# Gated attention and hash-routed experts on one core: routing in smaller parts, fetches at fixed steps, experts' matrices prepared from the third batch on

## The chip, the cores and the metric

The kernel runs on one core of one Trainium2 chip. A core has a matrix engine (PE, with its weight loads shown as PEld), a vector engine (DVE), an activation engine (ACT), a general engine (POOL) and a sync engine (SP); SP, ACT and POOL also issue the DMAs here, each in its own program order. The metric is the device time of one execution in microseconds (us). Before the change three runs gave 2499.6, 2501.89 and 2503.09 us, median 2501.89 us.

## The reference: what is computed

Two stages. The attention has 8 batches of 2496 positions, with no softmax; its output, 19968 rows of 256, is the input of the second stage, in which each row goes through one of 8 experts, chosen by the low three bits of its token's number (the hash's factor leaves 1 when divided by 8).

```python
scores = (1/S) * z @ z.T            # z: 8 x 2496 x 64
attn   = maximum(scores, 0) ** 2
x      = u * (attn @ v)             # u, v: 8 x 2496 x 256
# x as 19968 x 256
expert = token_ids % 8
out[expert == e] = maximum(x[expert == e] @ w1[e], 0) @ w2[e]   # 256 -> 1024 -> 256
```

## The kernel before

**Attention.** The sequence is cut in halves and each half in five groups of up to 256 positions. A step is one triple (batch b, group g of queries, tile s of keys): 25 steps for a batch, 200 in all, numbered i from 0. `STEPS` gives the order of s for each g, and pos = i % 5 is the place of a step in its group. A step makes the scores (`score`, L237: four matmuls of z at L250, ReLU and squares on ACT at L254 to L263, and on DVE at L259 on the diagonal), forms four sums of them on DVE (`sums`, L274 to L277), and multiplies them with v by the seven products of a two-by-two block scheme (`attend`, L325, 28 matmuls). Scores are symmetric. So a tile above the diagonal is also transposed on DVE (`mirror`, L290), written to HBM by SP (`keep`, L298 and L302), and read back by ACT's queue (`recall`, L306) instead of being computed when its mirror image is due. Scores and sums are made two steps ahead of their product (`AHEAD`), recalls are issued three ahead.

**Joins.** The seven products of a group collect over its five steps in four PSUM tiles, and there are only four such tiles. At pos 4 `join` reads them: ACT copies one product (L336), and DVE adds in seven instructions (L338 to L344). The next group's first product can't start before L336 and L338 are done.

**From a group to sorted rows.** One step after a join `gate` turns the result (L356); at pos 1 `put` stores it to HBM (SP, L363, four DMAs) and adds it to the list `waiting`. When the routing is known, `fetch` reads a waiting group back (SP: L371 or L375, and u at L222, three or four DMAs), `multiply` multiplies it by u five steps later (DVE, L388, four instructions), and `sort` writes each row to its slot with indirect DMAs (POOL, L410, four for a group). Of the buffers for u there are two, of those for the rows three.

**Next batch's z.** During a batch SP loads the next one's z in four pieces (`load_z`, L165, at steps 5, 9, 13 and 17 of the batch). Five steps after each load DVE turns the piece (`turn_z`, L185 and L187), and one step later SP copies it to the other half of the partitions (`copy_z`, L192, the last at step 23).

**Routing.** `places` is a generator: each `next` runs it to the following `yield`. It counts the rows of every expert, and gives every row a slot in blocks of 512, 256 or 128 rows of one expert. From step 5 on one part runs at the end of each step, 23 parts, the last at step 27. Only then do fetches begin, at any step with fewer than two groups in flight. From step 32 on one `enter` (POOL, L637) a step writes the token numbers into the slots, 160 in all.

**Experts' matrices.** Each of 16 half experts gets its sums for the seven products. `prepare` loads it (POOL, L659), adds on DVE in two parts of two instructions (L667 to L681), and stores it (POOL, L683); this starts at step 28 and repeats every ten steps, with the parts 0, 4, 5 and 7 steps after the load.

**The second stage** (from 1469 us) runs 60 blocks through the experts; the change touches nothing in it.

The order of instructions on each engine is the order in which this program issues them. At the end of a step it is: scores and sums for two steps on, `keep`, z, `attend`, `join`, `mirror`, v, `gate`, `put`, then routing or `multiply`, `sort` and `fetch`, then `enter` and `prepare`.

Of the kernel before, what the change touches and what calls it, by code (L numbers as in the profile page):

```python
# [24 lines left out]
def kernel(  # L25
# [12 lines left out]
    B, S, D = u.shape  # L38
    K = z.shape[-1]
    N = B * S  # L40
    E, _, F = moe_w1.shape
# [11 lines left out]
    BLK, MID = 512, 256  # L53
    TB, TM = BLK // P, MID // P
    NL = -(-(N - E * (BLK - 1)) // BLK)
    NM = -(-(N - NL * BLK - E * (MID - 1)) // MID)
# [10 lines left out]
    NT = -(-HS // (2 * P))  # L67
# [19 lines left out]
    C = B * 2 * T  # L87
# [342 lines left out]
    def places():  # L430

        with tc.tile_pool(name="route", bufs=1) as route:
# [137 lines left out]
            for size, spare, limit, name in ((BLK, 0, NL, "large"), (MID, 0, NM, "mid"), (P, P - 1, NR, "small")):  # L570
                n, end = share(count, size, spare, limit, name)
                more = route.tile([P, E], F32, name=name + "_more")
# [17 lines left out]
                if size == MID:  # L590
                    yield
# [3 lines left out]
            for (_, _, end), b0, nb in zip(levels, (0, NL, NBIG), (NL, NM, NR)):  # L595
                over = upto[0:1].rearrange(flat_e)[:, 0:nb * E].rearrange('p (j e) -> p j e', e=E)
                nc.vector.tensor_tensor(
                    over, end[0:1, :].unsqueeze(1).to_broadcast([1, nb, E]),
                    iota_b[:, 0:nb].unsqueeze(2).to_broadcast([1, nb, E]), op=OP.is_le)
                eb = route.tile([1, max(NL, NM, NR)], F32, name="eb")  # L600
                nc.vector.tensor_reduce(eb[:, 0:nb], over, axis=AX.X, op=OP.add)
                nc.vector.tensor_scalar(eb_i[:, b0:b0 + nb], eb[:, 0:nb], float(E - 1), None, op0=OP.min)
            nc.vector.tensor_tensor(eb_i[:], eb_i[:], most_i[0:1].to_broadcast([1, NB]), op=OP.bitwise_xor)
# [163 lines left out]
    PER = NG * NT  # L767
# [19 lines left out]
    PREP, PERIOD = 28, 10  # L787
# [12 lines left out]
    for i, (b, g, s) in enumerate(steps):  # L800
# [48 lines left out]
        if i >= 5 and not is_routed:  # L849
            is_routed = next(routed, True) is True  # L850
            if is_routed:

                rowpool = attention.enter_context(tc.tile_pool(name="rowpool", bufs=2))
        elif is_routed:
# [6 lines left out]
            if len(fetched) < 2 and waiting and (len(waiting) > 1 or i > put_at + 1):  # L861
                fetched.append((i, fetch(*waiting.pop(0))))
        if is_routed and 0 <= i - 32 < C:
            enter(i - 32)
        for part, after in enumerate((0, 4, 5, 7)):
            k, due = divmod(i - PREP - after, PERIOD)
            if not due and 0 <= k < 2 * E:
                prepare(k, part)
# [8 lines left out]
    assert is_routed and not waiting and not fetched  # L877
# [216 lines left out]
```

## Time and profile before

| what | value |
|---|---|
| median of three runs | 2501.89 us |
| the profiled execution's own time | 2505.98 us |
| its span (first to last instruction) | 2504.2 us |
| PE busy | 2474.7 us, 99% of the span |
| DVE, ACT, POOL busy | 1735.6, 722.8, 551.5 us |
| attention, about 14 to 1469 us | PE busy 1439.63 of the 1452 us from 17 to 1469 |
| a full step's 28 matmuls | 6.24 us in the chain (5.5 us in the fifth group, which is shorter) |

In a timeline each line has start, duration, engine, line, operation, what is written and read, and the number of instructions; in brackets stands how long the engine idled before it, and what ended that. A table by stretches gives busy time of each engine, then the TensorE clock that was granted (1.00 is full), the mean share of the 16 DMA engines, and GB/s. The step that runs at a time is found by counting L325's groups of 28 from 17 us on: step 20 starts at 169.0 us, step 30 at 243.1, step 45 at 353.0, step 50 at 392.6, step 70 at 541.7, step 100 at 755.1, step 125 at 935.7.

### The profile page before, as it was taken

The numbers are of one execution on the slowest core, as the hardware profiler recorded it, in microseconds if no ns is written. First come the engines' busy times: TensorE is split into PE (matmuls) and PEld (weight loads), VectorE is DVE, ScalarE is ACT, GpSimd is POOL, SyncE is SP. The second block draws the span as 40 slices with busy tenths as digits, with TensorE's granted clock in tenths as the row PEclk, the third lists the DMA queues.
The fourth block names the chain that finished last, engine by engine and source line by source line (L and its number), as shares of the span: only waits on it lengthen the run. The fifth ranks groups of instructions, "written<-read, shape, count | busy, mean of one in ns | idle before, by whom it ended". The sixth has DMA issues, their size and how long they took to land.

```text
span 2504.2 us, 37751 instructions
## 1 busy us (share of the span) xinstructions
PE 2474.7 (99%) x13751; PEld 2114.1 (84%) x13751; DVE 1735.6 (69%) x3686; ACT 722.8 (29%) x1231; POOL 551.5 (22%) x532
## 2 busy tenths in 40 slices
PE   8999999999999999999999999999999999999998
PEld 6787787787787787787777889999999999999998
DVE  7799768768768778778777666655665565556554
ACT  4314314314324224223233112222222222222221
POOL 0000243233313322332233211111111111121212
PEclk9999999999999999999999999999999999999999
DMA  7765798788788687797787776867676767667672
GB/s 147 181 177 161 209 283 235 200 266 220 215 247 228 204 255 201 236 268 195 236 251 210 240 248 208 281 213 215 205 256 192 263 193 252 211 228 232 213 247 75
DMA packets 437292, 550.70 MB, mean 220 GB/s; under 512 B 256908, under 2 KB 368861, under 8 KB 418928
## 3 DMA queue, kind: packets, MB, share of 16 engines
q1 hardware_dynamic: 377328, 363.19, 51.3%
q10 hardware_dynamic: 32448, 97.86, 11.4%
q0 software_dynamic: 27328, 87.23, 9.8%
q8 instruction: 108, 1.77, 0.3%
q14 instruction: 80, 0.66, 0.1%
HBM read 371.36 MB, written 173.24 MB: 217 GB/s over the span
## 4 chain that ended last, share of the span: by engine, by line
PE 87%; DMA 5%; DVE 5%; issue 1%; SPq 1%; ACT 0%; ACTq 0%; POOL 0%; POOLq 0%; DVEq 0%
PE acc L325 40%; PE o_ps L970 17%; PE h_ps L939 17%; PE s_ps L250 8%; PE h_ps L993 3%; PE o_ps L1004 3%; DMA a<-scores 2%; DMA zn<-in_z_dram 1%; DMA u_sb<-in_u_dram 1%; DVE mirror L290 1%; DVE t L274 1%; DVE t L276 0%; DVE t L275 0%; DMA v_sb<-in_v_dram 0%; DVE x_row L388 0%
## 5 line engine op out<-in xcount | busy, mean ns | idle before, releaser
L254 ACT ACTIVATE a<-s_ps 128x512 f32<-128x512 f32 (+1 forms) x480 | 246.6, 598 | 752.5 <-PE s_ps L250 730.1
L325 PEld LDWEIGHTS acc<-a,v_sb 128*128 128x128 f32 (+1 forms) x1600 | 294.6, 190 | 130.3 <-issue 44.5
L325 PE MATMUL acc<-t,vc 128*128 128x256 f32 (+3 forms) x1600 | 404.0, 375 | 0.0
L325 PE MATMUL acc<-a,v_sb 128*128 128x256 f32 (+3 forms) x1600 | 385.0, 383 | 9.6 <-DVE o L338 9.3
L410 POOL DMA_INDIRECT x_slots<-x_row,row x160 | 193.4, 1209 | 810.4 <-DVE x_row L388 671.8
L325 PE MATMUL acc<-t,v_sb 128*128 128x256 f32 (+3 forms) x1600 | 369.7, 373 | 0.0
L325 PEld LDWEIGHTS acc<-t,vc 128*128 128x128 f32 (+1 forms) x1600 | 304.5, 191 | 34.4
L325 PEld LDWEIGHTS acc<-t,v_sb 128*128 128x128 f32 (+1 forms) x1600 | 303.4, 190 | 33.7
L274 DVE TENSOR_TENSOR t<-a 128x512 f32<-128x512 f32 (+1 forms) x200 | 134.2, 671 | 228.6 <-ACT a L263 162.6
L939 PE MATMUL h_ps<-xs,w 128*128 128x256 f32 (+1 forms) x1248 | 288.4, 361 | 0.0
L970 PEld LDWEIGHTS o_ps<-w,h 128*128 128x128 f32 x2272 | 277.0, 192 | 7.9 <-DVE ro L903 1.2
L891 POOL DMA_INDIRECT out_dram<-o_sb,idx x142 | 143.4, 1010 | 629.9 <-issue 406.9
L970 PE MATMUL o_ps<-w,h 128*128 128x128 f32 x2272 | 280.4, 276 | 0.6 <-DVE ro L903 0.6
L250 PE MATMUL s_ps<-zT 64*128 64x512 f32 (+1 forms) x960 | 244.8, 623 | 10.8 <-DVE zT L185 8.0
L946 ACT ACTIVATE h<-h 128x512 f32<-128x512 f32 (+1 forms) x234 | 138.5, 592 | 352.8 <-DVE h L909 141.3
L939 PEld LDWEIGHTS h_ps<-xs,w 128*128 128x128 f32 x1248 | 208.2, 191 | 16.3
L290 DVE STREAM_TRANSPOSE mirror<-a 128x256 f32<-128x256 f32 x640 | 218.0, 407 | 2.0 <-DMA scores<-mirror 2.0
L939 PE MATMUL h_ps<-xT,w 128*128 128x256 f32 (+1 forms) x936 | 213.8, 361 | 2.5 <-DVE h L909 2.5
L970 PEld LDWEIGHTS o_ps<-w,hs 128*128 128x128 f32 x1704 | 206.9, 192 | 4.9
L970 PE MATMUL o_ps<-w,hs 128*128 128x128 f32 x1704 | 209.3, 275 | 0.0
L325 PE MATMUL acc<-a,vc 128*128 128x256 f32 (+3 forms) x800 | 202.0, 375 | 0.0
L637 POOL DMA_INDIRECT slot_tokens<-token,addr x160 | 168.1, 1051 | 65.9 <-issue 47.5
(177 smaller groups left out, 2638.6 us busy)
## 6 DMA issues: line engine op xcount, KB each, us to landing
w<-w_blocks SPq DMA_DIRECT2D x78, 1792.0 KB, 11.1
scores<-mirror SPq DMA_DIRECT2D x192, 256.0 KB, 4.4
a<-scores ACTq DMA_DIRECT2D x48, 1024.0 KB, 4.9
scores<-mirror SPq DMA_DIRECT2D x224, 128.0 KB, 3.8
a<-scores ACTq DMA_DIRECT2D x32, 896.0 KB, 5.7
w_blocks<-w POOLq DMA_DIRECT2D x16, 1792.0 KB, 7.6
w1s<-in_moe_w_dram SPq DMA_DIRECT2D x21, 1024.0 KB, 9.8
w2s<-in_moe_w_dram SPq DMA_DIRECT2D x21, 1024.0 KB, 16.4
```

The costliest lines, as they stand in the source:

```text
L250: nc.tensor.matmul(flat(ps)[:, 0:2 * w].rearrange("p (q c) -> p q c", q=2), tile_of_keys(b, h, s, j), q_h, start=True, stop=True)
L254: nc.scalar.activation(of[:, :, j, h].rearrange("p m q e -> p q m e"), flat(ps)[:, 0:2 * w].rearrange("p (q m e) -> p q m e", q=2, e=in_bl ...
L274: nc.vector.tensor_sub(t1, y12, y11)
L290: nc.vector.transpose(to, in_blocks(a, g)[:, :, j, h].rearrange("p i q (r t) -> p t i q r", t=2)[:, t])
L325: nc.tensor.matmul(acc[k][:, half, 0:w], x[0:n, j, :], y[0:n, j], start=(first and j == 0 and half == 0), stop=(last and j == 1), skip_gro ...
L410: st = nc.gpsimd.indirect_dma_start(out=x_dram[:, :], out_offset=bass.IndirectOffsetOnAxis(ap=row[0:m, c:c + 1], axis=0), in_=x_sb[0:m, q, ...
L637: st = nc.gpsimd.indirect_dma_start(out=slot_dram[:, None], out_offset=bass.IndirectOffsetOnAxis(ap=addr[0:n, to:to + 1], axis=0), in_=tok ...
L891: st = nc.gpsimd.indirect_dma_start(out=out[:], out_offset=bass.IndirectOffsetOnAxis(ap=idx[:, col:col + 1], axis=0), in_=o, in_offset=Non ...
L939: nc.tensor.matmul(ps[:, r], w1[j][:, k, ts(f + r, P)], y, start=first and r == 0, stop=True, skip_group_check=True)
L946: lambda o, i, k, ps=None: nc.scalar.activation(o, o if ps is None else ps, AF.Relu))
L970: nc.tensor.matmul(ps[:, t], x[:, f, ts(t, P)], w2_block(w2[j], k)[:, f], start=first and t == 0 and f == 0, stop=f == FQ - 1, skip_group_ ...
L993: nc.tensor.matmul(ps[:, i, :], w1[j][:, c, ts(f + i, P)], x[:, 0, c, 0:P], start=(c == 0), stop=(c == DP - 1))
```

## The change

Three things change in the order of the work; each engine gets the same instructions.

1. The routing is cut into 27 parts instead of 23 (a `yield` more after the first share, after each of the three sizes, and inside the loop over blocks). A part runs only at steps that are neither pos 4 nor in the first group of a batch: steps 5 to 8, 10 to 13, 15 to 18, 20 to 23, 30 to 33, 35 to 38 and 40 to 42. So the routing ends at step 42 instead of 27.
2. A waiting group is fetched only at steps 1, 5, 8, 12, 15, 19 and 22 of a batch (up to the last 25 steps, where the old rule holds). `multiply` still follows five steps later. `enter` starts when the routing is done and runs once a step, twice at pos 2.
3. `prepare` starts at steps -1, 3 and 8 of each batch from the third on (49, 53, 58, 74, ...), its parts 0, 3, 4 and 6 steps after that.

```diff
--- before.py
+++ after.py
@@ -569,6 +569,8 @@
             levels, base, added = [], 0, None
             for size, spare, limit, name in ((BLK, 0, NL, "large"), (MID, 0, NM, "mid"), (P, P - 1, NR, "small")):
                 n, end = share(count, size, spare, limit, name)
+                if limit == NL:
+                    yield
                 more = route.tile([P, E], F32, name=name + "_more")
                 nc.vector.tensor_sub(more[:], end[:], n[:])
                 nc.vector.tensor_scalar(more[:], more[:], float(size), float(base), op0=OP.mult, op1=OP.add)
@@ -587,8 +589,7 @@
                     nc.vector.tensor_add(next_first[:], first[:], taken[:])
                     first = next_first
                 base += limit * size
-                if size == MID:
-                    yield
+                yield
 
 
 
@@ -600,6 +601,8 @@
                 eb = route.tile([1, max(NL, NM, NR)], F32, name="eb")
                 nc.vector.tensor_reduce(eb[:, 0:nb], over, axis=AX.X, op=OP.add)
                 nc.vector.tensor_scalar(eb_i[:, b0:b0 + nb], eb[:, 0:nb], float(E - 1), None, op0=OP.min)
+                if nb == NM:
+                    yield
             nc.vector.tensor_tensor(eb_i[:], eb_i[:], most_i[0:1].to_broadcast([1, NB]), op=OP.bitwise_xor)
             nc.vector.tensor_scalar(eb_i[:], eb_i[:], E - 1, None, op0=OP.bitwise_and)
 
@@ -784,7 +787,13 @@
     LOAD_V = {-8: 0, -4: 1, -3: 2, -1: 3, 0: 4}
     ADD_V = {-5: 0, -2: 1, -1: 2, 1: 3, 2: 4}
     routed, is_routed = places(), False
-    PREP, PERIOD = 28, 10
+
+
+
+    ROUTE = [i for i in range(len(steps)) if i % NT != NT - 1 and i % PER not in range(NT)]
+    PREPARE = sorted(b * PER + x for b in range(2, B) for x in (-1, 3, 8))[:2 * E]
+    FETCH = (1, 5, 8, 12, 15, 19, 22)
+    entered = 0
     def prepare_mirror(i, a):
         if i < len(steps) and steps[i][2] > steps[i][1]:
             mirrors.append((*steps[i], mirror(*steps[i][1:], a)))
@@ -846,9 +855,10 @@
             late = closing["late"].enter_context(tc.tile_pool(name="late", bufs=1, side="right", reuse_waits="tile"))
             for j in range(SURE):
                 load_x(j)
-        if i >= 5 and not is_routed:
+        if i in ROUTE and not is_routed:
             is_routed = next(routed, True) is True
             if is_routed:
+                assert i < PREPARE[0] - 1
 
                 rowpool = attention.enter_context(tc.tile_pool(name="rowpool", bufs=2))
         elif is_routed:
@@ -858,14 +868,15 @@
                 to_sort += [(*rows, k) for k in range(4)]
             for _ in range(min(2, len(to_sort))):
                 sort(*to_sort.pop(0))
-            if len(fetched) < 2 and waiting and (len(waiting) > 1 or i > put_at + 1):
+            if len(fetched) < 2 and waiting and (i % PER in FETCH or i >= len(steps) - 5 * NT) and (len(waiting) > 1 or i > put_at + 1):
                 fetched.append((i, fetch(*waiting.pop(0))))
-        if is_routed and 0 <= i - 32 < C:
-            enter(i - 32)
-        for part, after in enumerate((0, 4, 5, 7)):
-            k, due = divmod(i - PREP - after, PERIOD)
-            if not due and 0 <= k < 2 * E:
-                prepare(k, part)
+        for _ in range((1 + (i % NT == 2)) * is_routed):
+            if entered < C:
+                enter(entered)
+                entered += 1
+        for part, after in enumerate((0, 3, 4, 6)):
+            if i - after in PREPARE:
+                prepare(PREPARE.index(i - after), part)
         if i == len(steps) - 20:
             load_w(0, 0)
         if i == len(steps) - 2:
@@ -874,7 +885,7 @@
             load_u(b, g)
         if i == len(steps) - 4:
             load_u(b, g, late)
-    assert is_routed and not waiting and not fetched
+    assert is_routed and not waiting and not fetched and entered == C
     for _ in range(len(to_sort)):
         sort(*to_sort.pop(0))
 
```

## The prediction

> **What bounds the kernel now.** I read the page first, then busy time by stretches, then PE's timeline for its idle stretches, then what DVE and SP did ahead of them.
>
> ```profile
> PE 2474.7 (99%) x13751; PEld 2114.1 (84%) x13751; DVE 1735.6 (69%) x3686; ACT 722.8 (29%) x1231; POOL 551.5 (22%) x532
> ...
> PE 87%; DMA 5%; DVE 5%; issue 1%; SPq 1%; ACT 0%; ACTq 0%; POOL 0%; POOLq 0%; DVEq 0%
> ```
>
> ```profile
> 17.00:1469.00 1452.00, 1439.63 (x6553) 1140.39 (x6553) 1122.84 (x2502) 449.39 (x709) 379.56 (x347) 1.00 0.77 221
> ...
> 1490.00:2494.00 1004.00, 1003.42 (x7065) 949.70 (x7064) 591.56 (x1142) 257.59 (x497) 158.92 (x158) 1.00 0.67 221
> ```
>
> PE is the bound, and the change takes no matmul away. The second stage stands still for 0.6 us in 1004. All that can be won is idle time of PE in the attention, 1452 - 1439.63 = 12.4 us, and what a lowered clock adds. These are its idle stretches:
>
> ```profile
> 124.75 1.14 PE L250 MATMUL s_ps<-zT 64*128 64x512 f32 x4 [0.68 <-ACT a L254]
> 169.01 2.47 PE L325 MATMUL acc<-a,v_sb 128*128 128x224 f32 x8 [2.52 <-DVE o L338]
> 243.06 1.99 PE L325 MATMUL acc<-a,v_sb 128*128 128x256 f32 x8 [0.70 <-DVE o L338]
> 352.99 2.15 PE L325 MATMUL acc<-a,v_sb 128*128 128x224 f32 x8 [2.05 <-DVE o L338]
> 388.87 3.75 PE L250 MATMUL s_ps<-zT 64*128 64x512 f32 x6 [2.11 <-DMA zT<-zT]
> 541.65 1.78 PE L325 MATMUL acc<-a,v_sb 128*128 128x224 f32 x8 [1.26 <-DVE o L338]
> 755.07 1.99 PE L325 MATMUL acc<-a,v_sb 128*128 128x256 f32 x8 [0.82 <-DVE o L338]
> 935.66 1.99 PE L325 MATMUL acc<-a,v_sb 128*128 128x256 f32 x8 [1.01 <-DVE o L338]
> 1262.33 1.78 PE L325 MATMUL acc<-a,v_sb 128*128 128x224 f32 x8 [0.78 <-DVE o L338]
> ```
>
> All but the first and the zT one are joins: PE waits for L338, which stands behind other work in DVE's order. Three of them are followed by a slow clock (the last three columns: granted clock, DMA share, GB/s):
>
> ```profile
> 170.00:174.00 4.00, 4.00 (x14) 3.68 (x13) 3.86 (x7) 0.00 (x0) 0.00 (x0) 0.58 0.56 147
> 354.00:358.00 4.00, 4.00 (x15) 3.63 (x14) 3.86 (x10) 0.00 (x0) 3.08 (x4) 0.57 0.75 280
> 388.00:392.00 4.00, 3.13 (x6) 1.20 (x6) 3.93 (x13) 1.05 (x2) 3.09 (x4) 0.55 0.72 169
> 392.00:396.00 4.00, 4.00 (x11) 2.85 (x11) 3.52 (x11) 2.64 (x4) 2.03 (x3) 0.60 1.03 373
> ```
>
> A clock of 0.58 over 4 us loses (1 - 0.58) x 4 = 1.7 us; the others lose 1.7, and 1.8 + 1.6 = 3.4. Idle stretches of 2.05 us and more had it, those of 1.26 and less had not.
>
> Now what stood ahead. At 352.99 and 541.65 it was a `multiply` at pos 3 that waited for its u, at the zT stall a crowded SP queue:
>
> ```profile
> 346.86 0.43 DVE L388 TENSOR_TENSOR x_row<-x_row,u_sb 128x256 f32<-128x256 f32 x1 [2.60 <-DMA u_sb<-in_u_dram]
> 349.03 0.68 DVE L680 TENSOR_TENSOR w<-w 128x512 f32<-128x512 f32 x1
> ...
> 533.34 0.77 DVE L185 STREAM_TRANSPOSE zT<-zn 64x256 f32<-64x256 f32 x2 [4.37 <-DMA zn<-in_z_dram]
> 537.15 0.43 DVE L388 TENSOR_TENSOR x_row<-x_row,u_sb 128x256 f32<-128x256 f32 x1 [2.76 <-DMA u_sb<-in_u_dram]
> ```
>
> ```profile
> 364.76 5.85 SPq L371 DMA_DIRECT2D x_row<-x  x1
> 370.72 3.35 SPq L222 DMA_DIRECT2D u_sb<-in_u_dram  x2
> 376.66 0.47 SPq L192 DMA_DIRECT2D zT<-zT  x1
> ```
>
> **The change part by part.** The instructions of each engine are the same; only places differ, so each term is an idle stretch that goes, stays or comes.
>
> *Routing.* Ahead of 169.01 DVE ran the shares of step 17 and, from 161.37 to 166.29, those of step 18 and the block numbers: 4.9 us of instructions of 0.17 to 0.41 us, then sums, then L338 at 168.54, while PE was free at 166.5. Now step 17 has the scan (L541, 2.78 us) and step 18 one addition (L544, 1.45 us); the shares lie at 20 to 23, the block numbers at 30 and 31. From step 15 to this join DVE has about 26.5 us by its rows (sums 2.2 to 2.7 each, a mirror 2.7, the join's rest 2.8, the routing 6.3), PE about 34 (five products of 6.24 us and two sets of scores). The stall goes: -2.5 - 1.7 = **-4.2**. The last part (L625, 2.37 us, and four small ones), which sat ahead of the join at 243.06, goes to step 42, with a step free before its join: **-0.7**. At step 24 L338 had 1.1 us to spare; the four parts at 20 to 23 are 8.5 us against 5.8, but DVE idled 2.6 us at 199.5 before it: 0 to +1.5, I take +0.3. The three counting rounds move from steps 12, 13, 14 to 13, 15, 16; each holds two score banks until DVE has copied them, and now two rounds stand ahead of a step with scores, not one: **+0.7**, one more stall like that at 124.75 (0 to +1.4).
>
> *Fetches.* In steps 28 to 48 nine fetches were issued; now there are two, at 44 and 47. So no `multiply` stands ahead of the join at 352.99, and no preparing addition (L680, L681: 1.3 us): -2.05 - 1.7 = **-3.8**. The zT copy of step 48 had fetches 38, 39, 43 and 44 ahead of it on SP, of which one took 5.85 + 3.35 = 9.2 us there; now it has 44 and 47: -2.11 - 3.4 = **-5.5**.
>
> Later, `multiply` leaves pos 18 and 23, the steps ahead of the last two joins of a batch: it runs at 6, 10, 13, 20 and 24 (there after the join), and while the backlog lasts (eight groups at step 42, seven fetches a batch against five new groups, so to about step 133) at 2 and 17 too. A `multiply` is 1.43 us by its row, and its wait for u 2.76 at 537.15. The stalls at 541.65, 755.07, 935.66 and 1262.33 and 0.2 at 574.84: 1.26 + 0.82 + 1.01 + 0.78 + 0.2 = **-4.1**. Joins at step 14 keep their `multiply` at 13 and their 0.3 us.
>
> What is late next: seven fetches a batch put more on SP, and SP's DMAs share completion semaphores with ACT's, so some wait for recalls issued later in the program. In the changed order the store before `load_z` of step 63 (and 88, 113) waits for the recall of step 68; before it waited for v of step 67. In this profile that recall was issued at 524.02 and let SP on at 532.09, against 525.67 for the load. It should come sooner, at 529 to 532, with no z load beside it; z takes 6 to 7 us; DVE then needs 1.1 (L185, L187), 2.2 (sums) and 0.4 (L338): 539 to 543, where PE is ready at 540.4. So 0 to 2.6 us, and 1.7 of clock from about 2 on, at each of three joins: I take **+1.0** in all, near the low end, since DVE has lost the `multiply` there (ends 0 and +13). Its like at the batch's end: fetch 22 now stands right before the last zT copy (23). That copy lands 2.6 to 2.8 us after issue where nothing stands before it, 4.6 to 6.7 behind a fetch, and the fetch adds 1.5 us on SP (565.74 to 567.18). Before, it was issued at 563.56, 746.80 and 924.48, and PE's scores need it at about 572.7, 752.3 and 932.7. So 569.7 to 571.8, 752.9 to 755.0, 930.6 to 932.7: in time twice, late by 0.6 to 2.7 once. **+1.5** (0, to 9 each as the rival below). The recall of step 96, which was nearly late for its product (sums at 742.2, product at 746.8), hangs on SP's stores and keeps some of the 0.8 at 755.07: **+0.7** (0 to 2.5).
>
> *Preparing.* The additions move to steps 2, 3, 6, 7, 11 and 12, before joins that had 1.3 to 4.7 us to spare, so 0 (to +1.3, one pair of additions). The load has three steps, not four, before the first addition: 24 us, against a POOL queue that ran up to a step behind (313.6, step 39, for a load of step 38) and 7.6 us to land its like. POOL's `enter` moves from 32 to 191 to 42 to 174: POOL is 22% busy, nothing of PE waits for it.
>
> *Sum.* Gone: 4.2 + 0.7 + 3.8 + 5.5 + 4.1 = 18.3. Come: 0.3 + 0.7 + 1.0 + 1.5 + 0.7 = 4.2. Net -14.1 us: the profiled execution goes from 2505.98 to 2491.9. That execution was 4.1 us above the median, so on the median 2501.89 - 14.1 = **2487.8**.
>
> [...] Here 2.05 to 2.52 us idle were enough for a slow stretch. [...] The DMA engines were 0.98 busy from 375 to 395, when fetches crowded. [...]
>
> **Rivals.** *The fetches' crowd only moves.* In each of batches 2 to 4 the zT copy or the z of step 13 is late as at 388.87. For it: the semaphores above. Against: 7 fetches in 25 steps, not 9 in 21. With 4 us for each of three batches beyond my terms: 2488 + 12 = 2500, the same. *Slower: fetch 22 blocks the copy.* If it costs SP the 9.2 us of 364.76 and not 1.5, the copy lands 9.2 + 2 to 4 = 11 to 13 us later, against 2.8 to 4.6 to spare: 7 to 10 us idle and 1.7 to 3.4 of clock, say 10 at each of three batch ends: 2488 - 1.5 + 30 = 2516. It decides from a shift of about 10 us on (5 late, 3 of clock, three times, against the gain). Against: 372 us had two fetches at once and 0.98 of DMA. *Half the gain:* other waits (a<-scores came 10.5 us late to DVE at 742, unseen by PE) show once joins are quick: 2494.
>
> **Chances.** My sum, 2482 to 2491: 0.55. Half the gain, 2491 to 2496.9: 0.22. The crowd moves, 2497 to 2507: 0.13. Slower as above, over 2507: 0.10. What a measurement can tell from no change is 0.2%, 5 us; the third case I split 0.09 same and 0.04 slower. So faster 0.77, same 0.09, slower 0.14. The range 2480 to 2505 leaves out most of the last case and a little below.
>
> **What would show it.** Right: no idle PE at step 20's, 30's and 45's first product, zT in time at step 49, three clock dips fewer, no `multiply` right before joins 19 and 24. Wrong: PE waiting for zT or L338 at steps 70, 75, 95, 100, 120 or 125, after waits of DVE for z; or a dip there.

## The result, and the profile after

The changed kernel takes 2489.3 us (median of 15 runs, 2486.76 to 2499.0) against 2502.01 us for the kernel before (15 runs on the same chip, 2497.61 to 2505.36): a ratio of 0.9956, 95% interval 0.9945 to 0.9966. The forecast was 2487.8 us, with a range of 2480 to 2505. Its executions fall in two groups: eleven from 2486.8 to 2490.4 us and four from 2495.7 to 2499.0 us. The profiled execution is one of the upper group, 2499.0 us. A second profile of the same kernel, taken for the experiments, is of the lower one, 2488.28 us.

The page of the execution at 2499.0 us. PE's busy time is the same as before to 0.3 us. In the chain of work that ended last, PE's share rose from 87% to 95%, and DMA and DVE fell from 5% each to 2% and 1%:

```profile
PE 2475.0 (99%) x13751; PEld 2113.1 (85%) x13751; DVE 1734.0 (69%) x3686; ACT 723.1 (29%) x1231; POOL 553.3 (22%) x532
...
PE 95%; DMA 2%; DVE 1%; issue 1%; SPq 0%; ACT 0%; POOL 0%; POOLq 0%; ACTq 0%; DVEq 0%
```

PE's timeline of that execution, its idle stretches in the attention and the one at the change of stages:

```profile
108.38 1.12 PE L250 MATMUL s_ps<-zT 64*128 64x512 f32 x2 [0.35 <-DVE total L509]
139.48 1.61 PE L250 MATMUL s_ps<-zT 64*128 64x512 f32 x4 [0.68 <-ACT a L254]
742.53 3.75 PE L250 MATMUL s_ps<-zT 64*128 64x512 f32 x6 [4.09 <-DMA zT<-zT]
...
1475.61 2.07 PE L950 MATMUL h_ps<-xT,w 128*128 128x256 f32 x4 [2.32 <-DVE h L920]
```

No product waits for L338 any more: all seven stalls at joins have gone, and so has the one for zT at 388.87. One is new and large: at 742.53 PE waits 4.09 us for a copy of zT, and these stretches of the same trace (busy time of each engine, then granted clock, DMA share and GB/s) show what follows:

```profile
738.00:742.00 4.00, 0.44 (x2) 0.00 (x0) 3.86 (x11) 0.60 (x1) 0.00 (x0) 0.95 0.73 229
742.00:746.00 4.00, 3.47 (x6) 1.19 (x6) 3.97 (x13) 1.08 (x2) 0.00 (x0) 0.50 0.23 48
746.00:750.00 4.00, 4.00 (x10) 3.05 (x10) 2.02 (x5) 2.60 (x3) 3.12 (x3) 0.50 1.00 229
750.00:754.00 4.00, 4.00 (x15) 3.35 (x15) 3.96 (x11) 0.00 (x0) 3.19 (x4) 0.77 0.83 225
```

The clock lost over the four rows is 4 x (0.05 + 0.50 + 0.50 + 0.23) = 5.1 us. With the wait that makes 9.2 us, about what lies between the two groups; the three other executions of the upper group have no trace. SP's timeline of the same execution shows what stood ahead of the copy:

```profile
720.42 9.79 SPq L222 DMA_DIRECT2D u_sb<-in_u_dram  x2
730.31 2.91 SPq L363 DMA_DIRECT2D x<-x_sb  x4
733.40 0.38 SPq L371 DMA_DIRECT2D x_row<-x  x1
733.88 0.98 SPq L222 DMA_DIRECT2D u_sb<-in_u_dram  x2
734.95 0.90 SPq L192 DMA_DIRECT2D zT<-zT  x1
```

The copy is the last line. It belongs to step 98, whose first product ran at 724.4, and was issued 3.1 us after the first product of step 99 (731.8 us). Ahead of it on SP stand four stores of rows and a whole fetch, the one that the change put at step 22 of a batch, and ahead of these another u, whose two loads went out 9.5 us apart. SP's waits from 719 to 736 us (who waited for what: us in total, times, longest) put nearly all of that down to a load of v, which ACT had issued:

```profile
SPq L222 <- DMA v_sb<-in_v_dram: 9.1, 1, 9.1
```

The fetch of step 22 itself took SP 1.5 us, from 733.40 to 734.86. In the execution at 2488.28 us the same copy stood behind the same fetch and was issued at 731.34, 0.4 us after the first product of step 99, and the scores behind it took 3.21 us, where the same eight products took 2.00 in the run with the fetch behind the copy; so they were 1.2 us late there. PE's timeline of that execution:

```profile
736.46 3.21 PE L250 MATMUL s_ps<-zT 64*128 64x512 f32 x8
```

### The profile page after: what moved, and what is told of

It is laid out like the page before. It is cut to its first block, busy times and chain, and to the rows that moved or that the text cites. A ratio compares the mean times of both kernels' runs of the same rounds, so it can differ in the third digit from the quotient of the medians.

```text
span 2497.2 us, 37741 instructions
## 1 busy us (share of the span) xinstructions
PE 2475.0 (99%) x13751; PEld 2113.1 (85%) x13751; DVE 1734.0 (69%) x3686; ACT 723.1 (29%) x1231; POOL 553.3 (22%) x532
## 3 DMA queue, kind: packets, MB, share of 16 engines
q10 hardware_dynamic: 32448, 97.86, 11.9%
## 4 chain that ended last, share of the span: by engine, by line
PE 95%; DMA 2%; DVE 1%; issue 1%; SPq 0%; ACT 0%; POOL 0%; POOLq 0%; ACTq 0%; DVEq 0%
PE acc L325 46%; PE o_ps L981 17%; PE h_ps L950 17%; PE s_ps L250 9%; PE h_ps L1004 3%; PE o_ps L1015 3%; DMA a<-scores 1%; DMA zT<-zT 0%; DMA zn<-in_z_dram 0%; DVE mirror L290 0%; SPq L165 0%; DMA x<-x_sb 0%; DVE t L274 0%; DVE t L276 0%; DVE t L275 0%
## 5 line engine op out<-in xcount | busy, mean ns | idle before, releaser
L325 PE MATMUL acc<-t,vc 128*128 128x256 f32 (+3 forms) x1600 | 403.1, 374 | 0.0
L325 PEld LDWEIGHTS acc<-a,v_sb 128*128 128x128 f32 (+1 forms) x1600 | 294.3, 190 | 120.0 <-issue 53.5
L325 PE MATMUL acc<-a,v_sb 128*128 128x256 f32 (+3 forms) x1600 | 384.4, 383 | 0.1
L325 PE MATMUL acc<-t,v_sb 128*128 128x256 f32 (+3 forms) x1600 | 369.7, 373 | 0.0
L325 PEld LDWEIGHTS acc<-t,vc 128*128 128x128 f32 (+1 forms) x1600 | 304.0, 190 | 33.9
L325 PEld LDWEIGHTS acc<-t,v_sb 128*128 128x128 f32 (+1 forms) x1600 | 303.4, 190 | 33.6
L325 PE MATMUL acc<-a,vc 128*128 128x256 f32 (+3 forms) x800 | 201.3, 374 | 0.0
```

Source lines behind the costliest of these rows:

```text
L325: nc.tensor.matmul(acc[k][:, half, 0:w], x[0:n, j, :], y[0:n, j], start=(first and j == 0 and half == 0), stop=(last and j == 1), skip_gro ...
```

## The experiments

Each time stands beside the kernel before on the same chip. To compare profiles I worked out of each trace what every step loses: the time from its first product (L325) to the next step's, less what undisturbed steps of its kind need (6.05 us, 5.31 in the fifth group, and 2.12 or 1.88 more where new scores lie between). F are the fixed fetch steps, R the smaller routing parts at new steps, P the new steps for preparing. The versions made from the changed kernel (R and P, F and P) also have its steps for `enter`, those made from the kernel before (F, R or P alone) the old ones; `enter` was not tried by itself. The losses, in us, are those of one profiled execution, whose own time is in the second column; the columns leave out what all of them have, 0.3 us at a join in the middle of each batch and 0.9 at step 196.

| kernel | profiled | steps 11 to 16 and 17, 18 | joins 19, 29 | join 44 | ends of batches | other joins | sum of all |
|---|---|---|---|---|---|---|---|
| before | 2505.98 | 3.1 | 5.0 | 3.8 | 8.3 | 2.0 | 25.3 |
| F alone | 2507.09 | 3.1 | 3.2 | 0 | 18.4 | 0.9 | 28.2 |
| R alone (yields) | 2509.8 | 3.1 | 0 | 6.5 | 13.0 | 2.2 | 27.8 |
| P alone | 2494.22 | 3.1 | 3.1 | 1.5 | 0 | 2.3 | 14.0 |
| R and P | 2497.4 | 4.7 | 0 | 0 | 2.1 | 8.2 | 18.0 |
| F and P | 2492.15 | 3.1 | 4.9 | 1.4 | 1.8 | 0 | 13.7 |
| all, lower group | 2488.28 | 4.7 | 0 | 0 | 2.4 | 0 | 9.6 |
| all, upper group | 2499.0 | 4.7 | 0 | 0 | 11.7 | 0 | 18.9 |
| all, fetch a step later | 2488.12 | 4.7 | 0 | 0 | 0 | 0 | 7.4 |
| that, counting moved too | 2484.11 | 2.1 | 0 | 0 | 0 | 0 | 4.4 |

**The changed kernel again**, unedited, beside the next three.

> The changed kernel once more, for the same chip. Theory: its executions fall into two groups, because the last zT copy of a batch, which stands behind the fetch of step 22, is sometimes in time and sometimes not at step 99: most near 2488 us, some 8 to 10 us above, and a profile with or without an idle stretch of about 4 us <-DMA zT at step 100. Rival (the 4.09 us idle of the shown profile is a fixed cost of every execution): all executions within 4 us of each other, the idle stretch in every profile.

Measured: 2489.97 us (6 runs, 2487.05 to 2493.77) against 2503.62; ratio 0.9947 (0.9933 to 0.9961). The gain is there on another chip. The two groups are not: three executions lie at 2487.1 to 2488.3 us, two near 2491.8 and one at 2493.8, so neither the expected 8 to 10 us apart nor within the rival's 4 us. The one profile has no idle stretch ahead of step 100, which speaks against a fixed cost.

**The last fetch of a batch one step later**, so behind the last copy of zT on SP:

```diff
-    FETCH = (1, 5, 8, 12, 15, 19, 22)
+    FETCH = (1, 5, 8, 12, 15, 19, 23)
```

> Fetch at step 23 instead of 22 of a batch, so that it stands behind the last zT copy on SP and not before it; nothing else. Theory (the fetch delays the copy): no idle stretch <-DMA zT anywhere, the copy at the end of batch 3 is issued about 1.5 us sooner and lands about 3 us after issue instead of 7; time 2485 to 2489 us, executions within 5 us of each other. The multiply moves from step 2 to step 3, before a join with 1.3 to 2.6 us to spare: 0 to 1 us per batch with a backlog. Rival (chance landing of a DMA, whatever stands before it): the stretch and the executions near 2497 stay.

Measured: 2487.38 us (5 runs, 2486.57 to 2488.78); ratio 0.9935 (0.9921 to 0.9949), and no loss at any end of a batch in its profile.

**The copy of zT a step earlier**, in the step in which DVE turns the piece, so ahead of the fetch:

```diff
-            for after, do in ((0, load_z), (5, turn_z), (6, copy_z)):
+            for after, do in ((0, load_z), (5, turn_z), (5, copy_z)):
```

> The fetch stays at step 22, but every zT copy is issued in the step of its transposition, one step sooner, so the last one stands ahead of that fetch. Theory: as with the fetch moved, no idle stretch <-DMA zT, 2485 to 2489 us. If it is the number of fetches in the batch that makes the copy late, and not the one before it, the stretch stays and some executions are near 2497.

Measured: 2488.77 us (5 runs, 2486.84 to 2489.08); ratio 0.9937 (0.9923 to 0.9951), the ends of batches again at 0 in the profile. Either order that keeps the fetch from standing ahead of the copy takes the waits at batch ends away in the profile, 2.4 us in the unedited kernel's on this chip. The times alone do not show it: none of these ten runs is in the upper group, but none of the six unedited ones is either, and the ranges overlap. The difference of the two versions to each other is too small to tell.

**Fetches at any step, the other two edits kept (R and P):**

```diff
-            if len(fetched) < 2 and waiting and (i % PER in FETCH or i >= len(steps) - 5 * NT) and (len(waiting) > 1 or i > put_at + 1):
+            if len(fetched) < 2 and waiting and (len(waiting) > 1 or i > put_at + 1):
```

> The changed routing and preparing, but fetches at any step with fewer than two groups in flight, as before: eight waiting groups from step 43 on, ten fetches in 25 steps until about step 83. Theory (the crowd of fetches makes zT late and puts multiplies ahead of joins): stalls at joins 69, 94, 99, 119, 124 come back (4 us in all) and zT is late at the end of batch 2 or 1 (5 to 9 us): 2492 to 2502 us. Rival (the gain came from the routing alone and the fixed steps do nothing): 2487 to 2490 us.

Measured: 2497.4 us (9 runs, 2490.79 to 2499.03); ratio 0.997 (0.996 to 0.9981). Without the fixed steps 7 us of the gain are missing, and its profile has them at joins again (8.2 us, more than half of it at steps 119 and 120); of the late copy that was expected, 5 to 9 us, only 2.1 came. PE's and DVE's timelines there:

```profile
892.62 2.23 PE L325 MATMUL acc<-a,v_sb 128*128 128x224 f32 x8 [2.65 <-DVE o L338]
```

```profile
884.15 0.76 DVE L185 STREAM_TRANSPOSE zT<-zn 64x256 f32<-64x256 f32 x2 [5.59 <-DMA zn<-in_z_dram]
887.76 0.43 DVE L388 TENSOR_TENSOR x_row<-x_row,u_sb 128x256 f32<-128x256 f32 x1 [2.56 <-DMA u_sb<-in_u_dram]
...
892.16 0.41 DVE L338 TENSOR_TENSOR o<-r,acc 128x256 f32<-128x256 f32 x1
```

A multiply that waits for its u stands between a late z and the join, as at 541.65 in the kernel before. The fixed steps keep this place free.

**Fixed fetches alone**, put into the kernel before (F):

```diff
-            if len(fetched) < 2 and waiting and (len(waiting) > 1 or i > put_at + 1):
+            if len(fetched) < 2 and waiting and (i % PER in (1, 5, 8, 12, 15, 19, 22) or i >= len(steps) - 5 * NT) and (len(waiting) > 1 or i > put_at + 1):
```

> The kernel before with only the seven fixed fetch steps; routing in 23 parts up to step 27, preparing every ten steps as before. Theory: the idle stretches at 352.99 and 388.87 with their slow clock (9.3 us) go, those at later joins mostly go (4.1 us), those at 169.01 and 243.06 with theirs (4.9 us) stay, and zT is late at one batch end by chance (0 to 9): 2489 to 2496 us. Rival (the crowd at 350 to 390 us came from preparing beside the fetches, or from the routing's early end): the zT stretch at step 49 stays, 2497 us or more.

Measured: 2511.86 us (6 runs, 2507.09 to 2516.09) against 2501.82; ratio 1.0044 (1.003 to 1.0057). A miss: slower than the kernel before, as only the rival (2497 us or more) allowed. The wait at join 44 went, but the copy of zT at the end of the second batch came later still, 7.0 us after the first product of step 49 instead of 3.9. PE's, SP's and POOL's timelines of this run:

```profile
385.92 3.75 PE L250 MATMUL s_ps<-zT 64*128 64x512 f32 x6 [5.76 <-DMA zT<-zT]
```

```profile
358.43 12.68 SPq L222 DMA_DIRECT2D u_sb<-in_u_dram  x2
371.21 7.61 SPq L363 DMA_DIRECT2D x<-x_sb  x4
...
380.55 0.47 SPq L192 DMA_DIRECT2D zT<-zT  x1
```

```profile
360.28 0.60 POOL L683 DMA_DIRECT2D w_blocks<-w  x1
367.59 0.78 POOL L659 DMA_DIRECT2D w<-in_moe_w_dram  x1
```

The store of a prepared matrix (1792 KB) and the load of the next (1024 KB) are issued 7.3 us apart, both some 20 us or less ahead of the copy. The two loads of u and the four stores of rows that stand ahead of the copy on SP took 12.68 and 7.61 us. Nearly all of that is waiting for loads of v, which ACT had issued, to land; SP's waits from 356 to 382 us:

```profile
SPq L222 <- DMA v_sb<-in_v_dram: 11.9, 1, 11.9
SPq L363 <- DMA v_sb<-in_v_dram: 6.3, 3, 3.2
```

So the copy was held by landings on another engine's queue, with store and load among what the DMA engines had to move meanwhile. In the kernel before the store went out at 361.26 but the load only at 387.82, after the copy: POOL stood behind a scatter there, which began at 383.74 after 16.39 us of waiting. With other fetch steps POOL was free sooner, and the load moved ahead of the copy, to 367.59. How much of the 3.5 us more is the load's was not tried apart.

**Smaller routing parts alone** (R without its choice of steps: four more `yield`s in the kernel before, a part in every step):

```diff
+                if limit == NL:
+                    yield
...
-                if size == MID:
-                    yield
+                yield
...
+                if nb == NM:
+                    yield
```

> The kernel before with only the four more yields: 27 parts, one at every step from 5 to 31, also at joins. Theory (the long shares of steps 17 and 18 made the join at 169 late): that stretch and its slow clock go, 4.2 us; of the 0.7 at 243.06 some goes; 352.99 and 388.87 stay: 2496 to 2499 us. Rival (the place away from joins is what counts, not the size of the parts): the stretch at step 20 stays at 1 us or more and the time is 2500 to 2502 us.

Measured: 2501.84 us (12 runs, 2496.72 to 2510.08) against 2501.82; ratio 1.0002 (0.999 to 1.0013). A miss: no gain. The 5.0 us at joins 19 and 29 did go. But PE's timeline shows the next two waits grown from 2.05 and 2.11 us:

```profile
350.89 3.24 PE L325 MATMUL acc<-a,v_sb 128*128 128x224 f32 x8 [4.70 <-DVE o L338]
390.86 3.75 PE L250 MATMUL s_ps<-zT 64*128 64x512 f32 x6 [6.20 <-issue]
```

At the second of them the copy was issued 2.9 us after the first product of step 49, not later than in the kernel before, but the scores that need it began 9.9 us after its issue instead of 4.8. The store of a prepared matrix was 27 us ahead here, and the load went out 2 us behind the copy (382.93 after 380.97). So what is issued just behind the copy may count too; that was not tried apart. The profiled execution was among the slowest of its twelve, so the size of these two waits varies; that the gain is lost again shows in the median.

**A preparation every eight steps**, with the kernel before's spacing of the parts, in the changed kernel:

```diff
-    PREPARE = sorted(b * PER + x for b in range(2, B) for x in (-1, 3, 8))[:2 * E]
+    PREPARE = [49 + 8 * k for k in range(2 * E)]
...
-        for part, after in enumerate((0, 3, 4, 6)):
+        for part, after in enumerate((0, 4, 5, 7)):
```

> The changed kernel with preparing at steps 49, 57, 65, ... (every eight), with the old offsets 0, 4, 5 and 7, so that its additions fall on every place of a group, joins' too. Theory (its places cost nothing, the joins have room): as the changed kernel within 2 us, 2486 to 2491, with the same late zT at times. Rival (the chosen places 2, 3, 6, 7, 11, 12 matter): 1.3 us at each join that an addition precedes, some six of them: 2492 to 2497 us.

Measured: 2539.72 us (4 runs, 2534.58 to 2541.43); ratio 1.0146 (1.0127 to 1.0164). A miss of both theories, 2486 to 2497 us. The steps of preparing are far from free: of 60.8 us lost, 37.9 are at the ends of three batches (steps 74, 99 and 124) and 15.7 at joins and products of steps 114 to 179. PE's, POOL's and SP's timelines at the first of these ends:

```profile
565.90 3.75 PE L250 MATMUL s_ps<-zT 64*128 64x512 f32 x6 [7.42 <-DMA zT<-zT]
```

```profile
546.20 0.58 POOL L686 DMA_DIRECT2D w_blocks<-w  x1
...
548.07 0.95 POOL L662 DMA_DIRECT2D w<-in_moe_w_dram  x1
```

```profile
546.27 5.57 SPq L363 DMA_DIRECT2D x<-x_sb  x4
552.02 3.73 SPq L371 DMA_DIRECT2D x_row<-x  x1
...
559.01 0.58 SPq L192 DMA_DIRECT2D zT<-zT  x1
```

A store and a load right ahead of the copy, as in F alone; SP's queue is slow behind them (5.57 us for the stores of rows, and 3.73 for a load of rows, which the trace puts down to a wait for one of POOL's indirect DMAs), and the copy comes 7.8 us later than in the changed kernel (551.21).

**Counting rounds moved too.** The version with the fetch at 23, and no part of the routing at steps 11 and 15, so that the rounds that hold score banks sit elsewhere (the added 18 was in the list already):

```diff
-    ROUTE = [i for i in range(len(steps)) if i % NT != NT - 1 and i % PER not in range(NT)]
+    ROUTE = [i for i in range(len(steps)) if i % NT != NT - 1 and i % PER not in range(NT) and i not in (11, 15)] + [18]
```

> The changed kernel with the fetch behind the copy (step 23) and the routing's parts placed so that none of the counting products stands ahead of a step with scores: steps 11 and 15 are left out, so the total is at 12, the three rounds at 16, 17 and 18, and the routing ends at 45. Theory (the score banks held by the counts cost the 4.7 us that the steps 11 to 16 take beyond their matmuls, of which about 1.4 are the counting's own): 2 to 3 us below the kernel with the moved fetch alone, 2482 to 2486 us. Rival (those 4.7 us are DVE's load in that batch, wherever the counts stand): no difference to it.

Measured: 2485.1 us (6 runs, 2484.11 to 2485.82) against 2501.82; ratio 0.9932 (0.992 to 0.9944). The losses of steps 11 to 18 fell from 4.7 to 2.1 us, and the time is 2.3 us below the run with the fetch alone at 23 (on another chip). It is the best version of the study and faster than both kernels. All it still loses in the attention is 4.4 us. Its chain of work that ended last:

```profile
PE 98%; issue 1%; DMA 0%; DVE 0%; SPq 0%; POOL 0%; POOLq 0%; ACTq 0%; DVEq 0%
```

**New steps for preparing alone**, in the kernel before (P): `PREPARE` and the parts 0, 3, 4 and 6 in place of a start at step 28 and a period of ten.

> The kernel before, with the changed kernel's steps for preparing alone (steps 49, 53, 58, 74, ... and parts 0, 3, 4 and 6 steps later); routing parts and fetches as before. In the kernel before, the stretch from 360 to 388 us ahead of the late copy of zT has the DMA engines at a share of 0.96 to 1.13 in every 4 us, and the 1792 KB store of a prepared matrix is issued at 361.26 inside it. Theory A, the copy at a batch's end comes late by what else the DMA engines have to move in the 20 us or so ahead of it, so a store or load taken out of there comes back as time: the waits after steps 49 and 99 (6.3 and 0.9 us) go, and at 352.99 the part of the wait that the adds of preparing hold (some 2 us), 2493 to 2497 us. Theory B, the fetches of kept-back groups alone make the copy late, as the run of the changed kernel with fetches at any step (2497.4) suggests: 2499 to 2503 us, the wait after step 49 within 1 us of what it was.

Measured: 2499.17 us (12 runs, 2493.11 to 2503.33) against 2504.03; ratio 0.9974 (0.9961 to 0.9987). By the time alone this is theory B's range; by the difference to this chip's runs of the kernel before, -4.9 us, it is at the edge of A's. The profiled execution (2494.22 us, one of the fastest of the twelve) shows what A said: the 6.3 and 0.9 us after steps 49 and 99 are gone and join 44 lost 2.3 us less. SP's timeline ahead of the last copy of the second batch:

```profile
361.27 8.19 SPq L222 DMA_DIRECT2D u_sb<-in_u_dram  x2
...
376.68 0.52 SPq L192 DMA_DIRECT2D zT<-zT  x1
```

The crowd of fetches is there as before, with a u whose two loads take SP 8.19 us, and yet the copy is in time. In the 20 us or so ahead of it the store that was issued at 361.26 in the kernel before is the piece that is missing. P takes out more than that, though: the loads at 218 and 313.6 us and the store at 286.7 are gone too, so the store's own share is not shown by this run. Theory B falls for this execution; the spread of 10 us over the runs says that in others something still came late, and no trace of those was taken.

**The load two steps ahead of the batch's end**, in the best version:

```diff
-    PREPARE = sorted(b * PER + x for b in range(2, B) for x in (-1, 3, 8))[:2 * E]
+    PREPARE = sorted(b * PER + x for b in range(2, B) for x in (-2, 3, 8))[:2 * E]
```

> The version with the last fetch a step later and the counting rounds moved (2485.1), and the load that opens the preparation at each batch's end one step earlier: steps 48, 73, 98, 123, 148, 173 instead of 49, 74, ...; nothing else. With step 74 the load left GpSimd only at 566.27, after the joint of the batches, because GpSimd's queue stands behind the scatter of rows that waits for the last multiply; a step earlier it should leave at about 547, some 5 us ahead of the copy of zT. Theory A (the copy is late by the bytes queued ahead of it): 1024 KB at the 300 to 400 GB/s of these stretches are 2.6 to 3.5 us at each of six ends, less a slack of some 1 us, with up to 1.3 us of half clock behind: 1 to 5 us each, 2491 to 2510 us. Theory B (the run with a preparation every 8 steps lost its 50 us by its even spacing and its later adds, not by loads and stores ahead of the copies): 2484 to 2487 us.

Measured: 2486.81 us (4 runs, 2485.78 to 2488.64); ratio 0.9933 (0.9913 to 0.9954). The load left POOL at 543.39 instead of 566.27, as expected, but the time is B's. Of the six ends four lost nothing, two later ones 0.7 and 1.4 us. SP's timeline at the end where the load left at 543.39, and the four stores by themselves (shortest, median and longest issue in ns):

```profile
543.74 3.07 SPq L363 DMA_DIRECT2D x<-x_sb  x4
547.25 1.79 SPq L192 DMA_DIRECT2D zT<-zT  x1
```

```profile
L363 SPq DMA_DIRECT2D x<-x_sb x4: 302/357/487, 543.7 to 546.5; - x4
```

A load alone ahead of the copy fitted into the slack at four of the six ends; my price of 1 to 5 us at each end was too high.

**The routing as before, the other two edits kept (F and P):** the old parts, one at each step from step 5.

> The changed kernel with the old routing: its larger parts, one in every step from step 5 on, so fixed fetches and new steps for preparing without the smaller parts. With smaller parts alone the waits of 4.3 us after step 19 and 0.7 us after step 29 went, yet the whole was no shorter since the crowd at 350 to 390 us grew (17.8 us lost at steps 44 to 50 instead of 10.1). Theory A: with that crowd gone by the other two edits, the routing's own worth shows: 4.3 + 0.7 us come back, and the counting rounds beside scores (4.7 us against 3.1) go, 2492 to 2494 us against 2489 to 2490. Rival: the smaller parts matter for the crowd too, since they end the routing later and with it move when the kept-back groups are fetched: the waits at steps 44 to 50 come back, 2496 to 2500 us.

Measured: 2492.2 us (11 runs, 2490.55 to 2502.61) against 2504.03; ratio 0.9958 (0.9944 to 0.9972). As theory A had it, 2492 to 2494: the routing's own worth is there once the other two edits have taken the crowd away, 4.9 us at joins 19 and 29, of which 1.6 us go back to the counting rounds.

**A preparation every eight steps with the fetch behind the copy.** The run at 2539.72 with `FETCH` ending in 23 and the counting rounds moved.

> A preparation every 8 steps from step 49 (parts 0, 4, 5 and 7 steps later), as in the run at 2539.7, but with the last fetch a step later, so behind the copy of zT on SyncE's queue, and with the counting rounds moved; nothing else differs from that run. There 37.9 us were lost at the ends of three batches (steps 74, 99, 124) and 15.7 us at multiplies of steps 114 to 179. Theory A, bytes ahead of the copy: the 1792 KB store and the 1024 KB load that stood right ahead of it there are 6.9 to 8.2 us at the 350 to 420 GB/s of those stretches wherever the fetch stands, less the slack of some 3 us that the 1024 KB alone did not use up: still 4 us and more at each of the three ends, with the clock's share 15 to 30 us in all; 2510 to 2530 us. Theory C, the order on SyncE's queue: only because a fetch that is held up by those bytes stood ahead of the copy did the copy come late; with the fetch behind it less than 8 us are lost at the three ends and the 15 us at the multiplies stay; 2495 to 2508 us.

Measured: 2528.12 us (4 runs, 2527.45 to 2530.75) against 2502.63; ratio 1.0102 (1.0084 to 1.012). Theory A by time and by place: 25.5 us at the three ends (37.9 before), and 7.9 at a fourth, step 149. PE's, POOL's and SP's timelines:

```profile
558.19 2.58 PE L250 MATMUL s_ps<-zT 64*128 64x512 f32 x6 [2.94 <-DMA zT<-zT]
```

```profile
541.67 0.59 POOL L686 DMA_DIRECT2D w_blocks<-w  x1
...
543.64 0.96 POOL L662 DMA_DIRECT2D w<-in_moe_w_dram  x1
```

```profile
542.75 8.42 SPq L363 DMA_DIRECT2D x<-x_sb  x4
551.26 2.53 SPq L192 DMA_DIRECT2D zT<-zT  x1
```

Nothing of a fetch stands between the stores of rows and the copy here. The stores took 8.42 us to go out instead of the 3.07 of the run with the load alone, and the copy itself 2.53 instead of 1.79. One of the four stores makes the difference:

```profile
L363 SPq DMA_DIRECT2D x<-x_sb x4: 328/1106/5744, 542.8 to 549.9; - x4
```

The run is 12.4 us better than the one with the fetch ahead, each against its own comparison (25.5 us behind the kernel before, not 37.9), of which the counting rounds have 2.3; so the order on SP is worth some 10 us, and 33 us are still lost at the ends of batches, beside the matrices that are moved meanwhile. The stretches of this run show the DMA engines full (columns as above, the last three the granted clock, the DMA share and GB/s):

```profile
540.00:544.00 4.00, 4.00 (x21) 3.02 (x20) 2.34 (x5) 0.00 (x0) 3.39 (x5) 1.00 1.03 371
544.00:548.00 4.00, 4.00 (x21) 3.13 (x21) 2.22 (x5) 3.14 (x6) 0.60 (x1) 1.00 1.10 440
```

But a full share is not what sets them apart. In the run with the load alone the DMA engines are as good as full over the same stretches (0.96 and 1.00), and only the bytes are fewer:

```profile
544.00:548.00 4.00, 4.00 (x21) 3.31 (x21) 3.83 (x8) 1.58 (x3) 0.36 (x1) 1.00 1.00 299
```

What only the slow run has ahead of its copy, among the transfers of this size, is the 1792 KB store at 541.67.

**What the parts are worth.** By medians against the kernel before on the same chip: R alone 0.0 us, F alone +10.0, P alone -4.9, R and P -6.2, F and P -11.8, all three -13.7 (in the first comparison -12.7). The sum of the single ones would be +5.1. So the fixed fetches cost 10 us with the old steps for preparing, and gain 7 with the new ones; preparing gains 5 with the old fetches and 22 with the fixed ones. Each of these differences holds for the pair it names; R alone lacks the choice of steps that the changed kernel has. Routing and fetches without the new steps for preparing were not tried.

## Why the prediction was right, and where not

The time and the sign were right: -14.1 us forecast, -12.7 and -13.7 measured. Step by step, against the two profiles of the changed kernel:

- *Routing, -4.2 and -0.7:* 4.3 and 0.7 us went in every profile with the smaller parts. Right in place and size, though worth nothing alone.
- *Join 44, -3.8:* gone, all 3.8 us. Right for the whole change. It was put down to the `multiply` for the greater part: F alone takes it all away, P alone leaves 1.5 of it. But F and P with the old routing leave 1.4, so it is not the `multiply` alone.
- *The zT copy at 388.87, -5.5:* 6.3 us went, but this is the step that failed in its reason. The prediction saw the fetches ahead of the copy on SP as the cause, took 9.2 us as what one of them had cost, and gave preparing nothing. Of these 9.2 us 5.85 are one load of rows, and the trace puts them down to a wait for one of POOL's scatters; POOL issued two, at 362.18 and 363.47, right behind the store of a prepared matrix, 1792 KB. POOL's timeline and SP's waits from 361 to 385 us in the kernel before:

```profile
361.26 0.61 POOL L683 DMA_DIRECT2D w_blocks<-w  x1
```

```profile
SPq L371 <- DMA x_slots<-x_row,row: 5.9, 1, 5.9
```

  In P alone, without that store, the load of rows at 360.68 took 0.41 us. F alone made this very wait worse, 9.8 us instead of 6.3, with fewer fetches. In three pairs of profiles, one execution each, the new steps for preparing take it away or nearly: 6.3 to 0 (before and P), 11.2 to 0 (R, and R and P), 9.8 to 1.3 (F, and F and P). So preparing is tied to it whatever the fetches do. Which of the loads and stores that P moves counts for how much is open.
- *Preparing, 0 (to +1.3):* the failed term by size. It is -4.9 alone and -21.8 next to the fixed fetches. I priced the additions on DVE and asked whether the load arrived in time for them; I did not ask what the load and the store keep waiting.
- *Later joins, -4.1:* the stalls at 541.65 and 1262.33 went, 2.0 us by the steps' losses. The steps of the other two (99 and 124) kept 1.2 each, now as scores that wait for zT. So about 2.0 instead of 4.1, unless one counts the 2.4 us under the next term.
- *Fetch 22 ahead of the copy, +1.5:* 2.4 us in the lower group, 11.7 in the profile of the upper group, of which 9.7 at one batch end: the price of 10 us that the slower rival gave to each of three ends. So the rival's size was real at one end of one profiled execution; the others of the upper group have no trace. Its reason was not: the fetch itself cost SP the 1.5 us of the sum, and 9.1 us went to a wait for a load of v ahead of it. With the fetch behind the copy the loss is 0, and the median is 2.6 us lower, with ranges that overlap.
- *Steps 70, 95 and 120, +1.0 (0 to 13):* nothing. DVE does wait for z there, 5.4 to 7.0 us in the profile at 2499.0, but L338 is done 0.7 to 1.6 us ahead of PE. With a preparation every eight steps the same wait grew to 13.53 us and the join at step 169 lost 7.8:

```profile
1278.77 0.76 DVE L185 STREAM_TRANSPOSE zT<-zn 64x256 f32<-64x256 f32 x2 [13.53 <-DMA zn<-in_z_dram]
```

  (DVE's timeline of the last run.) So the risk was rightly placed, and the changed kernel is 0.7 us away from it. The semaphores that the term was argued from are in the trace of the kernel before: 1175 DMAs of SP and 168 of ACT end on the same eight.
- *Counting rounds, +0.7 (0 to 1.4):* 4.7 us against 3.1, so +1.6, past the end of the range. The total's product, now at step 11, stands ahead of a step with scores too (1.4 us lost there, 0.9 before), which the sum left out, and of the two rounds there the second cost 1.7; moving them gave the expected gain.
- *Recall of step 96, +0.7, and join 24, +0.3:* nothing lost at either; join 24 kept its 1.1 us to spare.
- *The lowered clock:* the prediction let every idle stretch of 2.05 us and more cost a slow stretch. At 2.05 to 2.52 us the runs show it sometimes there and sometimes not (below), so the 6.8 us of clock in the sum are what that one execution had, not what each has.

In all, the terms that failed cancel: preparing was given 0, and the gain that the runs tie to it was in the sum already, under fetches. That the sum came out so near is luck as far as the copy of zT goes: the size was read from the rows, the reason was not. The forecast held because all three edits came together; for any one edit alone by the same sum, it would have been wrong by 4 to 20 us (fetches: -13.4 + 3.2 = -10.2 forecast, +10.0 measured; routing: -3.9 and 0.0; preparing: 0 and -4.9).

## What to carry to other kernels

Before a transfer on the critical path is moved or cleared, list what every engine's queue puts on the DMA engines in the 20 us ahead of it, bulk moves of other stages first: with a 1792 KB store and a 1024 KB load there 33 us were lost, and the order of the queue that issues the late copy was worth some 10. Read a queue's slow stretch by what it waited for, too, and not by the transfer that stands there: here it was often a landing on another engine's queue (a load of v that ACT had issued, for 9.1 of 9.79 us in the changed kernel and 11.9 of 12.68 in F alone). Edits that clear the same stretch are not to be priced one by one: a part can cost 10 us alone and gain 7 with its partner. And a queue that runs behind hides where its loads go out; whoever makes it faster moves them: with the fixed fetches alone POOL's load went out at 367.59 us instead of 387.82, ahead of the late copy.

## What the runs showed of the hardware

- **The clock's drop was not a matter of the idle time alone.** The stall ahead of step 20 was nearly the same in four kernels, 2.46 to 2.52 us. After it the clock fell in the kernel before (0.58 over 170 to 174 us) and in F and P, and did not in P alone and F alone. PE's timeline and the stretch behind it, of P alone:

```profile
168.27 1.78 PE L325 MATMUL acc<-a,v_sb 128*128 128x224 f32 x8 [2.48 <-DVE o L338]
```

```profile
168.00:172.00 4.00, 3.73 (x19) 3.59 (x20) 3.90 (x9) 0.00 (x0) 0.00 (x0) 1.00 0.58 217
```

  and of F and P:

```profile
168.34 2.92 PE L325 MATMUL acc<-a,v_sb 128*128 128x224 f32 x7 [2.46 <-DVE o L338]
```

```profile
168.00:172.00 4.00, 3.66 (x10) 3.33 (x11) 3.90 (x9) 0.00 (x0) 0.00 (x0) 0.57 0.50 205
```

  The same wait costs some 1.8 us more or not: 5.0 us at joins 19 and 29 in the kernel before and 4.9 in F and P, 3.1 in P alone and 3.2 in F alone (table above). In all fourteen traces, from 40 us on, PE idled 20 times for 0.9 to 1.74 us, and no slow stretch followed; 22 times for 2.05 to 2.52 us, and one followed 13 times; 14 times for 2.65 us or more, and one followed each time. At the change of stages every kernel idles 2.3 to 2.5 us, with a slow stretch in seven of the fourteen traces, and for the changed kernel in one of its two. Apart from the one at each execution's end, the slow stretches, at a granted clock of 0.50, last 3.41, 6.83, 10.24 or 13.65 us, that is 3.41 or two to four times as much (3.41 and 6.83 us in the kernel before, 3.41 and 10.24 in the changed one). Why the same wait has a slow stretch behind it in one trace and not in another is not shown.
- **Behind a 1792 KB store, single small transfers got stuck as they were issued, for up to 5.74 us; full DMA engines alone did not do that.** I counted the DMAs that SP issued from 180 to 1455 us in all fourteen traces, leaving out those during whose issue a semaphore moved that they wait for: 8569, with a median of 0.48 us. Only 17 took more than 3 us, up to 5.74 (the store of rows above). Of the 17, 12 start less than 8 us behind a 1792 KB store of POOL's, where only 661 of the 8569 start, and 4 of these 12 have no load of 1024 KB in the 20 us before them; so it does not take the load. Behind a load without a store it was 2 of 590. Of the 1776 at a DMA share above 0.95 with neither in the 20 us before, none took more than 2.2 us. Why a store holds the issue is not shown. The store was POOL's, and what was held stood on SP's own queue, with all that was behind it: in the last run the stores of rows took 8.42 us and the copy went out at 551.26, against 3.07 us and 547.25 in the run with the load alone.
